# Placing attention units, token mixing and loads among MLP matmuls by planned matmul time, and beginning the second batch's units while its loads still arrive

## Chip, cores and metric

The kernel runs on one core of one Trainium2 chip. The metric is device time in microseconds (us), the median over several runs. Every kernel is compared with the kernel before on the same chip.

## The reference

Four batches of 768 tokens, 8 heads of 48, so a model width of 384. First a decaying attention:

```python
for t in range(S):
    kt, vt, rt = (k[:, :, t], v[:, :, t], r[:, :, t])
    cur = np.einsum('bhd,bhe->bhde', u[None] * kt, vt)
    y[:, :, t] = np.einsum('bhd,bhde->bhe', rt, state + cur)
    state = w[None, :, :, None] * state + np.einsum('bhd,bhe->bhde', kt, vt)
```

Then a mixer: one product over tokens (hidden width 256), one over channels (hidden width 1536), each with a residual:

```python
xt = x.transpose(0, 2, 1)
h = np.maximum(xt @ w_tok1, 0.0) @ w_tok2
u = x + h.transpose(0, 2, 1)
h2 = np.maximum(u @ w_ch1, 0.0) @ w_ch2
return (u + h2)
```

Token mixing needs all 768 tokens of a batch, so the channel MLP of a batch cannot begin before the attention of that whole batch is done.

## The kernel before

The attention goes in 24 "units" of 128 tokens: units 0 to 5 are batch 0, 6 to 11 batch 1, and so on. A unit passes through four stages, one per "slot". Slot `s` runs them for four neighbouring units, so that each engine has another unit's work while one waits:

```python
STAGES = ((3, stage_c), (2, stage_b), (1, stage_a), (0, stage_p))

def slot(s, lo, hi):
    for lag, f in STAGES:
        if lo <= s - lag < hi:
            f(*units[s - lag])
```

The profile calls the engines PE (TensorE, the matrix products), DVE (VectorE), ACT (ScalarE), POOL (GpSimd) and SP (SyncE, which here issues the loads, the stores and the transposing DMAs). In the timelines PE's products and the operations of DVE, ACT and POOL start in the order in which the Python code calls these functions, so this order is the schedule of each engine. The lines, by stage:

```python
# stage_p (units of batch 1 on): POOL, POOL, ACT, POOL
pool.tensor_mul(kp[:, :, 0:D], h3(kt), h3(wn[:, g, :]))      # `dve if early` cut
pool.tensor_mul(rp[:, :, 0:D], h3(rt), h3(wp[:, g, :]))
act.copy(vb, vt)
pool.tensor_mul(ku, kt, u_bc)
# stage_a: eight transposes on PE (cut), then
act.copy(L["rk"], tr_ps)
dve.tensor_mul(rku, L["ku"], L["rt"])
dve.tensor_reduce(adg, h3(rku), axis=mybir.AxisListType.X, op=ALU.add)
# stage_b: yd on POOL, eight products on PE (cut), two mask products AT on DVE (cut)
pool.tensor_mul(h3(L["yd"]), h3(L["vb"]), L["adg"].unsqueeze(2).to_broadcast([128, H, D]))
# stage_c: products into y_ps and kv_ps on PE (cut), then the state S and x_b on DVE (cut)
```

So POOL has four products a slot (yd, kp, rp, ku), and DVE has rku, adg, two AT, S and x_b, seven operations with an osb or a u_sb where one falls into the slot. Token mixing, the two MLP halves, and their DVE parts:

```python
def back(c):
    hT_ps = psM.tile([128, dm], f32, name="hT_ps", tag="m")
    for i in range(2):
        pe.matmul(hT_ps, wtok2[:, i, ts(c, 128)], h1r[:, i, :], start=(i == 0), stop=(i == 1))
    dve.tensor_add(u_sb[:, c, :], x_b[:, c, :], hT_ps)
    if not by_pe:
        sp.dma_start_transpose(uT[:, :, ts(c, 128)], u_sb[:, c, :])

def up(b, sg, jt):      # cut: three matmuls of uT into z_ps (tag "m"), then
    return act.activation(zr[:, jt, :], z_ps, Relu)

def down(b, sg, si):    # cut: twelve matmuls of zr into h2_ps (tag "m"), then
    dve.tensor_add(osb, mixed[b][0][:, c, :], h2_ps)
    sp.dma_start(out[b, ts(c, 128), :], osb)
```

All of z_ps, h_ps, hT_ps and tr_ps share one ring of four buffers (tag "m") in PSUM, where PE's products are written. A matmul group that opens a new buffer waits until DVE or ACT has read the one four places back.

For the first batch's MLP the order was a list of ups and downs with hand-set positions:

```python
items = ([None] * 6 + ups[6:16] + [downs[0]] + ups[16:20] + [downs[1]] + ups[20:] + downs[2:5] + [None])
slot_at = dict(zip(range(6, 16), (14, 17, 19, 21, 23, 25, 26, 27, 28, 28)))
load_at = (1, 3, 5, 7, 9, 11, 18, 20, 22, 24, 25, 26, 27)
tok_at = (28, 29, 29)
```

Slot 7, the first with a transpose of batch 1, stands behind ten ups and a down: ups[6:16] are items 6 to 15, the down is item 16, and slot 7 goes ahead of item 17.

## Time and profile before

| | before |
|---|---|
| median of 3 timed runs | 190.89 us (190.28 to 191.17) |
| span of the profiled run | 188.6 us, mean clock 0.98 |
| PE busy | 163.5 us (87%), 1434 instructions |
| DVE / ACT / POOL busy | 116.9 (62%) / 87.3 (46%) / 95.2 (50%) us |
| first up of batch 1, 2, 3 | 90.20, 125.61, 157.60 us |
| end of PE | 185.1 us |

The shares are averages over stages with different limits, so the row to read is the time of the first up of batch 1: ahead of it PE has gaps, from there on it has almost none.

### The profile page before, as it was taken

To read this page: it belongs to the slowest core of one execution; us is meant where nothing else is said; L and a number is where in the kernel's file an instruction comes from. 1 tells how busy PE (TensorE), PEld (TensorE's weight loads), DVE (VectorE), ACT (ScalarE), POOL (GpSimd) and SP (SyncE) were. 2 spreads that over 40 slices of the span, in tenths; PEclk is the share of its full clock that TensorE was granted. 3 is DMA by queue.
4 is the path that set the end of the run, shared out by engine and by line. 5 is a ranking of instruction groups with operands and counts; after the bars stand their busy time and mean duration, and the time that the engine had idled before them with its cause. 6 is when DMAs were issued, how large, how long until landed. Compare 5 with 4: busy or idle time off the path is not lost.

```text
span 188.6 us, 3783 instructions
## 1 busy us (share of the span) xinstructions
PE 163.5 (87%) x1434; PEld 104.4 (55%) x1434; DVE 116.9 (62%) x204; ACT 87.3 (46%) x168; POOL 95.2 (50%) x114
## 2 busy tenths in 40 slices
PE   5456579899998696895899999899999999999992
PEld 2255465366665464553666666466666666666661
DVE  4599997430599999939577874967765261111121
ACT  4933341479575344313556653534454525445510
POOL 5799998700299999966456772656410000000000
PEclk9999999999999999589999999999999999999999
DMA  6999999997999979404399744232011124211112
GB/s 128 215 191 218 180 211 199 186 188 149 222 222 213 215 157 239 105 0 104 66 217 200 159 114 100 71 70 80 0 45 42 42 48 116 92 42 45 73 52 83
DMA packets 90070, 24.03 MB, mean 127 GB/s; under 512 B 83267, under 2 KB 90053, under 8 KB 90053
## 3 DMA queue, kind: packets, MB, share of 16 engines
q1 hardware_dynamic: 86240, 20.65, 50.7%
q0 software_dynamic: 3808, 3.15, 10.7%
q8 instruction: 11, 0.18, 0.4%
q14 instruction: 7, 0.05, 0.1%
q10 hardware_dynamic: 4, 0.00, 0.0%
HBM read 20.45 MB, written 4.72 MB: 133 GB/s over the span
## 4 chain that ended last, share of the span: by engine, by line
PE 54%; SPq 19%; POOL 10%; DVE 6%; issue 4%; DMA 3%; ACT 1%; POOLq 0%; DVEq 0%
PE h_ps L68 26%; SPq L68 19%; PE z_ps L68 18%; PE tr_ps L68 3%; POOL yd L68 2%; PE y_ps L68 2%; POOL rp_129 L68 2%; DVE u_sb L68 2%; PE hT_ps L68 2%; POOL kp_130 L68 2%; DMA vt<-in_v_dram 2%; DMA uT<-u_sb 1%; DVE rku L68 1%; POOL rp_125 L68 1%; POOL rp_121 L68 1%
## 5 line engine op out<-in xcount | busy, mean ns | idle before, releaser
L68 ACT ACTIVATE zr<-z_ps 128x384 bf16<-128x384 f32 x96 | 43.9, 495 | 26.1 <-PE z_ps L68 26.1
L68 PE MATMUL z_ps<-uT,wch_149 128*128 128x384 bf16 x288 | 52.0, 326 | 3.2 <-DMA uT<-u_sb 2.7
L68 PE MATMUL h_ps<-wch_150,zr 128*128 128x384 bf16 x288 | 50.5, 326 | 0.0
L68 ACT COPY rk<-tr_ps 128x1024 bf16<-128x1024 bf16 x24 | 24.3, 1012 | 53.0 <-PE tr_ps L68 52.7
L68 DVE TENSOR_TENSOR osb<-u_sb,h_ps 128x384 f32<-128x384 bf16 x24 | 13.3, 553 | 50.8 <-PE h_ps L68 50.8
L68 PEld LDWEIGHTS <-zr 128*128 128x128 bf16 x288 | 28.1, 98 | 19.4 <-issue 1.5
L68 PEld LDWEIGHTS <-wch_149 128*128 128x128 bf16 x288 | 27.3, 98 | 20.0 <-issue 3.6
L68 POOL TENSOR_TENSOR yd<-vb,adg 128x384 f32<-128x384 bf16 x24 | 20.7, 862 | 28.8 <-DVE adg L68 16.4
L68 DVE TENSOR_TENSOR rku<-ku,rt 128x384 f32<-128x384 f32 x24 | 25.5, 1060 | 1.6 <-POOL ku L68 1.6
L68 POOL TENSOR_TENSOR ku<-kt,u_bc 128x384 f32<-128x384 f32 x24 | 24.5, 1022 | 0.0
L68 PEld LDWEIGHTS <-rk 48*128 48x128 bf16 (+1 forms) x272 | 12.5, 105 | 6.2 <-ACT rk L68 2.8
L68 DVE TENSOR_REDUCE adg<-rku 128x8 f32<-128x384 f32 x24 | 13.3, 553 | 0.8
L68 ACT CAST vb<-vt 128x384 bf16<-128x384 f32 x24 | 12.3, 513 | 0.0
L68 PE MATMUL hT_ps<-h1r,wtok_148 128*128 128x384 bf16 x48 | 9.4, 325 | 0.8 <-ACT h1r L68 0.4
L68 POOL TENSOR_TENSOR rp_121<-rt,wp 128x384 bf16<-128x384 f32 x8 | 8.9, 1112 | 2.3 <-ACT wp L68 2.3
L68 POOL TENSOR_TENSOR kp_126<-kt,wn 128x384 bf16<-128x384 f32 x6 | 6.0, 996 | 6.5 <-issue 5.9
L68 POOL TENSOR_TENSOR rp_129<-rt,wp 128x384 bf16<-128x384 f32 x8 | 8.9, 1114 | 0.0
L68 POOL TENSOR_TENSOR rp_125<-rt,wp 128x384 bf16<-128x384 f32 x8 | 8.6, 1073 | 0.0
L68 PEld LDWEIGHTS <-wtok_147 128*128 128x128 bf16 x48 | 5.6, 120 | 5.1 <-issue 3.5
L68 POOL TENSOR_TENSOR kp_122<-kt,wn 128x384 bf16<-128x384 f32 x6 | 6.0, 997 | 4.3 <-issue 3.6
L68 ACT ACTIVATE h1r<-h_ps 128x384 bf16<-128x384 f32 x8 | 3.5, 488 | 9.3 <-PE h_ps L68 9.3
L68 PEld LDWEIGHTS <-wtok_148 128*128 128x128 bf16 x48 | 4.7, 98 | 4.5 <-issue 1.8
(306 smaller groups left out, 231.5 us busy)
## 6 DMA issues: line engine op xcount, KB each, us to landing
kt<-in_k_dram SPq DMA_DIRECT2D x24, 192.0 KB, 3.6
rt<-in_r_dram SPq DMA_DIRECT2D x24, 192.0 KB, 3.7
vt<-in_v_dram SPq DMA_DIRECT2D x24, 192.0 KB, 3.7
out_dram<-osb SPq DMA_DIRECT2D x24, 192.0 KB, 2.0
wch_149<-in_moe_w_ch_dram POOLq DMA_DIRECT2D x3, 384.0 KB, 8.6
wch_150<-in_moe_w_ch_dram POOLq DMA_DIRECT2D x1, 1152.0 KB, 16.7
wtok_147<-in_moe_w_tok_dram POOLq DMA_DIRECT2D x1, 384.0 KB, 7.8
wtok_148<-in_moe_w_tok_dram POOLq DMA_DIRECT2D x1, 384.0 KB, 7.1
```

The lines of the kernel that those rows point to most:

```text
L68: return lambda *args, **kw: tc.keep_in_program_order(f(*args, **kw))
```

## The change

The intent: give every piece a planned PE cost (an up 0.5 us, a down 2.0, a slot 1.4), and give each slot, mixing step and load a planned time at which it is set among the ups and downs. In the stretch of batch 0's MLP, slots 6, 7 and 8 now come first, while the loads of their units still arrive; the slots follow every 4.2 planned us; mixing of batch 1 is split into its hidden product (H) and two halves of the second product (K1, K2) with slots between them; and one slot and one down more are done before batch 1's first up. Positions in the later batches change too. No operation is added or removed. The core of the diff:

```diff
-            items = ([None] * 6 + ups[6:16] + [downs[0]] + ups[16:20] + [downs[1]] + ups[20:] + downs[2:5] + [None])
-            slot_at = dict(zip(range(6, 16), (14, 17, 19, 21, 23, 25, 26, 27, 28, 28)))
-            load_at = (1, 3, 5, 7, 9, 11, 18, 20, 22, 24, 25, 26, 27)
-            tok_at = (28, 29, 29)
 ... (the loop that walked these positions, removed)
+    def merge(items, events):
+        now, events = 0.0, sorted(events, key=lambda e: e[0])
+        for cost, f in items:
+            while events and events[0][0] <= now:
+                _, c, g = events.pop(0)
+                g()
+                now += c
+            f()
+            now += cost
+        for _, _, g in events:
+            g()
+    UP, DOWN, SLOT = 0.5, 2.0, 1.4
 ... (helpers att, mixing, ups, downs, woven, fetch)
+    u1 = ups(0, 1)
+    items = ups(0, 0, 6) + u1[:6] + downs(0, 0, 0, 1) + u1[6:] + downs(0, 0, 1) + downs(0, 1)
+    events = [att(0.0, 6), att(0.0, 7), att(1.5, 8)] + [att(6.0 + 4.2 * j, 9 + j) for j in range(6)]
+    events += mixing(1, 27.5, 30.0, 32.0) + [att(29.0, 15), att(31.0, 16)]
+    merge(items, fetch([0.0] * 6 + [12.0, 16.0, 20.0, 24.0, 26.0, 27.0]) + events)
+    for b in range(1, B):
+        dn = downs(b - 1, 1) if b > 1 else []
+        items = (woven(ups(b, 0), dn) if dn else ups(b, 0)) + woven(ups(b, 1), downs(b, 0))
+        span = sum(c for c, _ in items)
+        events = []
+        if b + 1 < B:
+            at = [0.0, 5.5, 11.0, 16.0, 22.0, 28.0] if b == 1 else [0.0, 6.0, 12.0, 18.0]
+            events += [att(t, (17 if b == 1 else 23) + j) for j, t in enumerate(at)]
+            total = span + 4.0 + SLOT * len(at)
+            events += mixing(b + 1, total - 8.0, total - 4.5, total - 2.0)
+            events = fetch([0.0, 5.0, 10.0, 15.0, 20.0, 25.0]) + events
+        merge(items, events)
```

The stretch is written as a list of words, in the order in which the functions are called: S6 is slot 6, U4 four ups, D a down, H, K1 and K2 as above; loads are left out of the lists. The two kernels are:

```
before:  U8 S6 U2 D S7 U2 S8 U2 S9 D U1 S10 U2 S11 U1 S12 D S13 D S14 S15 H D K1 K2
changed: S6 S7 S8 U4 S9 U6 S10 U2 D S11 U5 S12 U1 D D S13 D S14 H S15 K1 S16 K2 D D
```

More of the change, by code (lines that the diff above doesn't have):

```diff
@@ L378 @@
         tn[3 + c]()
-    for b in range(B):
-        if b == 0:
-            ups = [lambda jt=jt, sg=sg: up(0, sg, jt) for sg in range(2) for jt in range(NJ)]
-            downs = [lambda sg=sg, si=si: down(0, sg, si) for sg in range(2) for si in range(3)]
-            items = ([None] * 6 + ups[6:16] + [downs[0]] + ups[16:20] + [downs[1]] + ups[20:] + downs[2:5] + [None])
-            slot_at = dict(zip(range(6, 16), (14, 17, 19, 21, 23, 25, 26, 27, 28, 28)))
-            load_at = (1, 3, 5, 7, 9, 11, 18, 20, 22, 24, 25, 26, 27)
-            tok_at = (28, 29, 29)
-        else:
-            items = []
-            for sg in range(2):
-                for si in range(3):
-                    if sg == 1 or b > 1 or si == 2:
-                        items.append(lambda si=si, b=b, sg=sg: down(b - 1 + sg, 1 - sg, si))
-                    items += [lambda jt=4 * si + j, sg=sg, b=b: up(b, sg, jt) for j in range(4)]
-            m = len(items)
-            slot_at = {6 * b + 10 + j: m - 30 + 5 * j + 1 for j in range(6)}
-            if b == 1:
-                slot_at[16] = 0
-            load_at = range(0, m, 5)
-            tok_at = (m - 8, m - 5, m - 2)
-        toks = None
-        for n in range(len(items)):
-            for x in load_at:
-                if x == n:
-                    load_next()
-            for s, x in slot_at.items():
-                if x == n:
-                    slot(s, C, len(units))
-            if b + 1 < B:
-                if n == tok_at[0]:
-                    toks = token_mix(b + 1)
-                    for f in toks[0]:
-                        f()
-                if n == tok_at[1]:
-                    for f in toks[1][:3]:
-                        f()
-                if n == tok_at[2]:
-                    for f in toks[1][3:]:
-                        f()
-            if items[n]:
-                items[n]()
@@ L422, with att @@
-    for si in range(3):
-        down(B - 1, 1, si)
+    def merge(items, events):
[10 more added lines that the diff above has]
+    UP, DOWN, SLOT = 0.5, 2.0, 1.4
+    def att(t, s):
+        return (t, SLOT, lambda: slot(s, C, len(units)))
@@ new lines, in mixing, with ups, downs, woven @@
+    def mixing(b, t_hid, t_bk1, t_bk2):
+        hid, bk, _ = token_mix(b)
+        go = lambda fs: [f() for f in fs]
+        return [(t_hid, 2.0, lambda: go(hid)), (t_bk1, 1.0, lambda: go(bk[:3])),
+                (t_bk2, 1.0, lambda: go(bk[3:]))]
+    def ups(b, sg, lo=0, hi=NJ):
+        return [(UP, lambda jt=jt: up(b, sg, jt)) for jt in range(lo, hi)]
+    def downs(b, sg, lo=0, hi=3):
+        return [(DOWN, lambda si=si: down(b, sg, si)) for si in range(lo, hi)]
+    def woven(us, ds):
+        out = []
+        for i, d in enumerate(ds):
+            out += [d] + us[4 * i:4 * i + 4]
+        return out
@@ new lines, in fetch @@
+    def fetch(times):
+        return [(t, 0.0, load_next) for t in times]
+    u1 = ups(0, 1)
[15 more added lines that the diff above has]
+        merge(items, events)
@@ L425 @@
+    for _, f in downs(B - 1, 1):
+        f()
 _INS = ['r', 'k', 'v', 'w', 'u', 'moe_w_tok1', 'moe_w_tok2', 'moe_w_ch1', 'moe_w_ch2']
```

## The prediction

> **What bounds the kernel now.** I read the page first, then the busy time by stretch, the chain of waits, and the timeline of POOL. Some names for pieces of work, by the tiles that they write: an "up" is three matmuls into z_ps, a "down" is twelve of zr into h_ps, A is the eight transposes of a unit into tr_ps, B its eight products into at_ps, C its state and output products into y_ps and kv_ps. Units 0 to 5 belong to batch 0, 6 to 11 to batch 1, and so on. A slot s does C of unit s-3, B of s-2, A of s-1, and P of s (the products kp, rp, ku on POOL).
>
> ```profile
> PE   5456579899998696895899999899999999999992
> POOL 5799998700299999966456772656410000000000
> PEclk9999999999999999589999999999999999999999
> DMA  6999999997999979404399744232011124211112
> ```
>
> The reader sees three regimes. The DMA is full until about 75 us, PE has gaps until about 90 us, and from there PE is full to the end. POOL stops for some 14 us at slices 8 to 10 (counted from 0) and is then full.
>
> ```profile
> core 0: us, PE busy (x) PEld busy (x) DVE busy (x) ACT busy (x) POOL busy (x), PEclk, DMA share, GB/s
> 41.70:53.70 12.00, 11.50 (x107) 7.27 (x105) 4.46 (x8) 10.01 (x22) 3.14 (x4) 1.00 0.98 190
> 53.70:77.50 23.80, 18.63 (x233) 12.74 (x233) 23.59 (x39) 10.40 (x17) 23.80 (x25) 0.95 0.99 210
> 77.50:90.20 12.70, 9.93 (x72) 5.91 (x73) 9.79 (x19) 3.72 (x6) 8.58 (x9) 0.82 0.16 41
> 90.20:185.10 94.90, 94.01 (x778) 59.27 (x778) 47.89 (x84) 44.47 (x91) 27.83 (x30) 1.00 0.35 85
> ```
>
> From 53.7 to 77.5 us POOL is busy 23.80 of 23.80 us, and DVE 23.59. Before that POOL has only 3.14 of 12.00.
>
> ```profile
> 35.55 0.99 POOL L68 TENSOR_TENSOR ku<-kt,u_bc 128x384 f32<-128x384 f32 x1
> 50.56 0.83 POOL L68 TENSOR_TENSOR yd<-vb,adg 128x384 f32<-128x384 bf16 x1 [14.03 <-DVE adg L68]
> 51.35 1.00 POOL L68 TENSOR_TENSOR kp_130<-kt,wn 128x384 bf16<-128x384 f32 x1
> 52.31 1.32 POOL L68 TENSOR_TENSOR rp_129<-rt,wp 128x384 bf16<-128x384 f32 x1
> 53.59 1.00 POOL L68 TENSOR_TENSOR ku<-kt,u_bc 128x384 f32<-128x384 f32 x1
> 54.55 0.83 POOL L68 TENSOR_TENSOR yd<-vb,adg 128x384 f32<-128x384 bf16 x1
> ```
>
> This is the costliest wait for the path: POOL stands in program order at yd of unit 6, which wants adg. The DVE pair that makes adg stands behind the first osb, so behind the first down, which PE ends at 48.7 us. From then on a slot takes four POOL products, and the starts of yd lie 54.55 - 50.56 = 3.99 us apart, with six more starts at 58.52, 62.49 up to 78.39: 3.97 each.
>
> ```profile
> 76.20 1.28 POOL rp_129 L68
> 77.52 0.61 PE tr_ps L68 x4
> 78.13 5.86 PE h_ps L68 x24
> 84.01 0.55 DVE osb L68
> 84.57 2.07 DVE u_sb L68 x5
> ...
> 87.72 2.34 DMA uT<-u_sb
> 90.07 0.14 issue
> 90.20 2.11 PE z_ps L68 x12
> ```
>
> The chain of waits shows what POOL's pace costs: PE waits for rp of unit 14, only then mixes batch 1, all six u_sb follow in one piece, then the transposing DMAs, and PE stands from about 87.5 to 90.2 us. From 90.2 us to 185.1 us PE is the bound.
>
> **What the Trainium skill says.** "SBUF — State Buffer", section "Who interferes with whom": a DVE instruction with two SBUF inputs contends with a POOL instruction that reads SBUF, and the second one blocks fully. The trace agrees: rku, two f32 inputs, takes 0.55 us at 49.25 with POOL idle and 1.34 us in most slots of the full stretch; rp there takes 1.28 instead of 0.96 us. So POOL and DVE cannot be counted as independent. "Perfetto Trace Analysis", section "Per-instruction lifecycle", GPSIMD part, advises to time POOL by start-to-start spacing, which I do. "TensorE: Matmul & The Clock Gate", Part 1, says that an idle window drops PE to half clock; here the clock is 0.82 in the stretch 77.5 to 90.2 and the 24 matmuls of the chain take 5.86 us where 24 take 3.9 us later. "DMA: Bandwidth & Descriptors", Specifications, wants runs of at least 512 B for line rate; the page has 83267 of 90070 packets under 512 B and about 200 GB/s while full, so I take the loads' landing times as they are.
>
> **The change, part by part.** No operation is added or removed; the order listing has the same number of instructions on every engine. Up to the last transpose of batch 0 (about 41.7 us on PE) the streams are the same.
>
> 1. Start of batch 1. Before, PE runs ten ups and a down ahead of A6. After, PE goes on with A6, B6, A7, four ups, then slot 9. On DVE rku and adg of unit 6 come right after the u_sb of batch 0, which end at 39.4 us, with no osb ahead. So yd6 is over by about 42 us. But the next POOL product is kp of unit 8, and its load is not there: by the completion times in the trace kt, rt and vt of unit 8 land at 45.1, 45.8, 46.6 us, unit 9 by 49.4, 10 by 52.2, 11 by 54.7. So kp8 starts at 45.1 instead of 51.35: POOL's pipeline moves forward by 6.2 us, not by the 14 us of the wait. After that loads (2.7 us a unit) are faster than POOL (3.97 us a slot). The load order up to unit 11 is unchanged.
>
> 2. PE's work in the stretch from 41.7 us to the first up of batch 1. Durations from the chain of waits: four ups 1.95, so 0.49 each; a down 1.95; C 0.54, B 0.33, A 0.55 (starts 92.31, 92.85, 93.18, 93.73); twelve matmuls of a first mixing product 1.95, three pairs of a second 0.97. Before, the stretch holds 18 ups (8.8), 5 downs (9.8), 10 A, 9 B, 8 C (12.8) and the mixing (3.9): 35.3 us of work in 90.2 - 41.7 = 48.5 us, so 13.2 us are gaps and half clock. After, it holds 18 ups, 6 downs (11.7), 11 A, 10 B, 9 C (14.2) and the mixing: 38.6 us.
>
> 3. How long it takes after. POOL's slots start at 48.2 + 3.97 (s - 9). I walk down PE's order with that, with the four buffers of the "m" psum ring, and with DVE at 0.47 to 0.6 us an operation: A8 at 47.6, A9 at 52, A10 56.4, A11 60.3, two downs to 64.7, A12 66.1, A13 69.5, first mixing product to 71.5, A14 73, three second products to 73.9, C13 waits for its mask product on DVE until 74.3, A15 waits for rp15 until 75.1. The last three second products and the first of two downs reach 79.4. The second down needs the psum of a second product, which DVE frees only after rku15 and adg15, at about 81.1, so it ends at 83.1, and slot 17 at 84.5. The transposing DMAs of the first three blocks are long done (u_sb at 77, landing about 81). So the first up of batch 1 is at 84.5, and 84.5 - 41.7 - 38.6 = 4.2 us of gaps are left.
>
> 4. The rest. Before, from 90.2: 72 ups (35.1), 19 downs (37.1), 8 A, 9 B, 10 C (12.8), two mixings (7.8): 92.8 us in 94.9, so 2.1 us of stalls. After: 72 ups, 18 downs (35.2), 7 A, 8 B, 9 C (11.3), two mixings: 89.4 us. The slots are set 4 to 6 us apart there, but for slots 22 and 23, with three second products and slot 22 between; DVE and POOL have half of the stretch free. I keep 2 us of stalls, and 3.5 us for the tail after PE.
>
> Sum: 84.5 + 89.4 + 2.1 + 3.5 = 179.5 us of span. The timed median is 2.3 us over the span of 188.6, so 181.8. The same from the difference: 13.2 - 4.2 = 9.0 us off 190.9 is 181.9. I round to 181.7.
>
> **Rivals.** (a) DVE becomes the bound. DVE was already at 23.59 of 23.80; after, six u_sb and six osb lie in the same stretch as the slots. For: in every slot with an osb DVE has almost no slack. Against: rku's 1.34 us is partly a wait for POOL, and slots with an osb kept 3.97. If every one of those twelve (0.47 each) pushed PE, 5.6 us come back: 186 to 187. (b) PE takes over at once and POOL's pace is hidden: 38.6 us without gaps, 177.6 us. For it: PE is then 90% loaded in the walk. (c) Loads hold it: the loads of units 12 on stand behind output stores in SP's order, which wait for osb. Against: at 3.97 us a slot unit 15 is wanted at 73 us, and the walk has it landed at about 71; at most 1 to 2 us. (d) The stretch loses to a drop of the PE clock: fewer gaps speak against it; one window as before would cost about 2 us. (e) Nothing gained, because the end is PE bound: no, since PE's gaps ahead of 90.2 us are a part of that sum.
>
> **Range and chances.** Rival (b) sets the low end, (a) with some of (c) the high end: 177.5 to 186.5. Faster by over 2% needs less than 187.1: 0.90. Within 2%: 0.08, if (a) and (c) come together. Slower: 0.02.
>
> **What would show it.** POOL's long wait of 14 us shrinks to under 4 us before yd6 plus a wait of some 3 us for kt before kp8 at about 45 us. The starts of yd are still near 4 us apart, from 48 to about 76. The first up of batch 1 comes at 82 to 87 us instead of 90.2, with one down and one slot more done. PE's clock stays near 1.00 from 42 to 85. From there to PE's end 90 to 93 us. I am wrong if yd's spacing grows past 4.3 us (DVE), if kp8 starts at 51 again (loads), or if the second half has over 4 us of stalls.

## The result

| | before | changed |
|---|---|---|
| median, us (4 runs of each) | 190.9 (190.28 to 191.17) | 185.47 (184.84 to 185.77) |
| profiled span, us | 188.6 | 183.1 |
| PE busy | 163.5 (87%) | 159.7 (87%) |
| DVE busy | 116.9 (62%) | 116.4 (64%) |
| POOL busy | 95.2 (50%) | 94.9 (52%) |
| first up of batch 1 | 90.20 | 86.76 |
| end of PE | 185.1 | 179.6 |

The ratio is 0.9716, with a 95% interval of 0.9679 to 0.9753: faster by 2.8%. Ratios here are the mean time of one kernel's fast runs over that of the other's of the same rounds, so they are not quite the ratio of the medians quoted. Executions over 1.5% slower than the fastest of the same kernel are left out of the means. PE's lower busy time is not less work: it has the same 1434 instructions, but the half-clock stretch from 75.1 to 82.0 us of the kernel before is gone.

Is the gain only this clock? By the record it can be a part, not all. Of the eleven runs of the kernel before that were made beside e5, those with a mean clock of 0.987 or 0.988 took 189.78 to 190.15 us, those with 0.980 to 0.982 took 190.62 to 191.46: about 1 us apart, for means that differ by one stretch of 3.4 us at half clock. By this estimate the 6.9 us above are worth some 2 of the 5.4 us. The four runs of the changed kernel have 0.988 to 0.999, and the one with the lowest clock is the fastest (184.84).

The slices of the changed kernel (one digit per 1/40 of the span, busy tenths; the last row the granted PE clock):

```profile
PE   5556579996999999677999999799999997999992
POOL 5799898905998877983668864770100000000000
PEclk9999999999999999999999999999999999999998
```

POOL's hole is now slice 8 and half of slice 9, and the clock is full up to PE's end. PE is still weak in slices 16 to 18 (6, 7, 7), which are 73 to 87 us. The same table of windows as before, with the two last edges moved to the new first up and the new end of PE:

```profile
core 0: us, PE busy (x) PEld busy (x) DVE busy (x) ACT busy (x) POOL busy (x), PEclk, DMA share, GB/s
41.70:53.70 12.00, 10.32 (x125) 7.21 (x124) 8.20 (x14) 10.28 (x21) 10.47 (x11) 1.00 1.08 207
53.70:77.50 23.80, 22.68 (x270) 15.69 (x268) 21.42 (x36) 11.65 (x23) 20.23 (x22) 1.00 0.83 176
77.50:86.80 9.30, 6.63 (x63) 4.24 (x63) 8.46 (x17) 1.41 (x2) 6.03 (x7) 1.00 0.27 55
86.80:179.60 92.80, 90.36 (x737) 56.83 (x734) 46.13 (x80) 45.35 (x91) 26.40 (x29) 1.00 0.38 93
```

From 53.7 to 77.5 PE now does 22.68 of 23.80 us (18.63 before) and POOL has slack (20.23). But from 77.5 to 86.8 PE is busy for only 6.63 of 9.30 us at full clock, while DVE is busy 8.46. POOL's timeline (start, duration, engine, operation, then in brackets the idle time before it and what ended that):

```profile
35.57 0.99 POOL L68 TENSOR_TENSOR ku<-kt,u_bc 128x384 f32<-128x384 f32 x1
43.23 0.83 POOL L68 TENSOR_TENSOR yd<-vb,adg 128x384 f32<-128x384 bf16 x1 [6.67 <-ACT vb L68]
44.02 1.00 POOL L68 TENSOR_TENSOR kp_130<-kt,wn 128x384 bf16<-128x384 f32 x1
...
66.14 1.00 POOL L68 TENSOR_TENSOR kp_126<-kt,wn 128x384 bf16<-128x384 f32 x1 [1.11 <-issue]
...
70.23 0.83 POOL L68 TENSOR_TENSOR yd<-vb,adg 128x384 f32<-128x384 bf16 x1 [1.17 <-DVE adg L68]
```

The wait of 14.03 us before yd of unit 6 has become one of 6.67, and what ends it is no longer adg from DVE but vb from ScalarE. ScalarE makes vb of unit 6 at 42.57 us, behind the last copy into uT, which starts at 42.21. kp of unit 8 starts at 44.02 without waiting: its load had landed at 42.7 in this run (45.1 in the profile before). yd then starts at 47.21, 51.19, 55.20, 60.22, 64.20, 70.23, 74.21, 78.18 and 83.05. Three spacings, 5.02, 6.03 and 4.87, are well over four us. DVE's timeline around the second:

```profile
65.70 0.55 DVE L68 TENSOR_TENSOR osb<-u_sb,h_ps 128x384 f32<-128x384 bf16 x1 [1.27 <-PE h_ps L68]
...
68.30 1.17 DVE L68 TENSOR_TENSOR rku<-ku,rt 128x384 f32<-128x384 f32 x1
69.50 0.55 DVE L68 TENSOR_REDUCE adg<-rku 128x8 f32<-128x384 f32 x1
```

Two downs stand in PE's order ahead of slot 13, so DVE gets the osb of each; at the second it is idle for 1.27 us waiting for PE, and S, x_b, two AT and then rku and adg stand behind it. adg is done at 70.05, so yd starts at 70.23 after 1.17 us of idle POOL. Work that POOL needs waits behind work that PE has not finished. A single down can do the same on a smaller scale: ahead of the spacing of 5.02, DVE waits 0.73 us for the down at 55.70. From the second osb on DVE has hardly a pause (the window has the columns of the table above; DVE's busy time is the third):

```profile
65.70:84.70 19.00, 15.23 (x177) 10.19 (x174) 18.86 (x32) 6.57 (x10) 15.39 (x16) 1.00 0.63 136
```

DVE is busy for 18.86 of 19.00 us, so each result there comes as late as all of DVE's work ahead of it makes it. On PE, close to the first up, that looks like this:

```profile
78.46 1.27 PE L68 MATMUL hT_ps<-h1r,wtok_148 128*128 128x384 bf16 x6 [1.06 <-DVE u_sb L68]
79.57 2.11 PE L68 MATMUL h_ps<-wch_150,zr 128*128 128x384 bf16 x12
83.39 2.11 PE L68 MATMUL h_ps<-wch_150,zr 128*128 128x384 bf16 x12 [1.71 <-DVE u_sb L68]
```

K2 (78.46) and then the second of the last two downs (83.39) wait 1.06 and 1.71 us for u_sb on DVE: going back four places in the PSUM ring, their buffers are those of the first products of K1 and of K2, which DVE has not yet read. (Gaps quoted below are counted from start to start, less the usual spacing; these two are then 1.23 and 1.87.) The chain of waits says the same from the other end:

```profile
81.46 0.84 DVE rku L68
...
82.79 0.56 DVE u_sb L68
...
83.39 2.11 PE h_ps L68 x12
```

DVE has rku, adg, u_sb in this order without a pause (rku 81.38 to 82.29, u_sb from 82.79), and PE starts its down right after the first u_sb. In the kernel before this part of the chain went through POOL's rp, then the half-clock downs and the transposing DMAs.

### The profile page after: what moved, and what is told of

It reads as the page before. It is cut to its first block, busy times and chain, and to the rows that moved or that the text cites.

```text
span 183.1 us, 3782 instructions
## 1 busy us (share of the span) xinstructions
PE 159.7 (87%) x1434; PEld 103.2 (56%) x1434; DVE 116.4 (64%) x204; ACT 87.5 (48%) x168; POOL 94.9 (52%) x114
## 4 chain that ended last, share of the span: by engine, by line
PE 70%; DVE 14%; ACT 4%; DMA 3%; issue 3%; SPq 1%; POOL 1%; DVEq 0%; POOLq 0%; ACTq 0%
PE h_ps L68 30%; PE z_ps L68 24%; PE tr_ps L68 4%; PE y_ps L68 3%; DVE rku L68 3%; PE hT_ps L68 3%; DVE u_sb L68 2%; DMA vt<-in_v_dram 2%; DMA kt<-in_k_dram 2%; PE kv_ps L68 1%; SPq L68 1%; ACT zr L68 1%; DVE x_b_151 L68 1%; PE w_ps L68 1%; ACT h1r L68 1%
## 5 line engine op out<-in xcount | busy, mean ns | idle before, releaser
L68 ACT ACTIVATE zr<-z_ps 128x384 bf16<-128x384 f32 x96 | 43.4, 498 | 31.1 <-PE z_ps L68 31.1
L68 PEld LDWEIGHTS <-wch_149 128*128 128x128 bf16 x288 | 27.4, 98 | 19.0 <-issue 2.4
L68 POOL TENSOR_TENSOR ku<-kt,u_bc 128x384 f32<-128x384 f32 x24 | 26.7, 1114 | 0.0
L68 DVE TENSOR_TENSOR rku<-ku,rt 128x384 f32<-128x384 f32 x24 | 24.7, 1028 | 1.6 <-POOL ku L68 1.6
L68 POOL TENSOR_TENSOR rp_121<-rt,wp 128x384 bf16<-128x384 f32 x8 | 8.0, 997 | 2.3 <-ACT wp L68 2.3
L68 POOL TENSOR_TENSOR rp_129<-rt,wp 128x384 bf16<-128x384 f32 x8 | 8.0, 996 | 0.0
L68 POOL TENSOR_TENSOR rp_125<-rt,wp 128x384 bf16<-128x384 f32 x8 | 8.0, 996 | 0.0
L68 PEld LDWEIGHTS <-wtok_148 128*128 128x128 bf16 x48 | 4.6, 99 | 5.1 <-issue 2.9
L68 POOL TENSOR_TENSOR kp_122<-kt,wn 128x384 bf16<-128x384 f32 x6 | 6.0, 996 | 2.8 <-PE kv_ps L68 2.8
L68 POOL TENSOR_TENSOR kp_126<-kt,wn 128x384 bf16<-128x384 f32 x6 | 6.0, 996 | 2.7 <-issue 2.3
L68 POOL TENSOR_TENSOR kp_130<-kt,wn 128x384 bf16<-128x384 f32 x6 | 6.0, 999 | 2.2 <-issue 2.1
```

Of the source, the lines that this page charges most:

```text
L68: return lambda *args, **kw: tc.keep_in_program_order(f(*args, **kw))
```

## The experiments

Every kernel has a profile and timed runs beside the kernel before on the same chip: three rounds for the first four (kernel before 190.04 us), five for the others (kernel before 190.65 us in both groups).

My theory after the result: the gain is in the stretch up to batch 1's first up, and what is left there (about 2.3 us against the prediction) is DVE's order, the prediction's rival (a). Rivals: the gain comes from placing the later batches; it comes from splitting the mixing rather than from the early begin; the remaining gaps come from PE's own order or the fill at 42 us.

### e1: the new stretch alone

```diff
-        items = (woven(ups(b, 0), dn) if dn else ups(b, 0)) + woven(ups(b, 1), downs(b, 0))
 ... (the planned times of b = 1, 2, 3, removed; the loop of the kernel before, put back with three changes:)
+                if (sg == 1 or b > 1 or si == 2) and not (b == 1 and sg == 0):
+            del slot_at[16]
+            slot_at = {s: max(x, 1) for s, x in slot_at.items()}
```

The changes leave out slot 16 and the down that the new stretch has already done.

> The changed order up to the mixing of batch 1, the order of before from batch 1's ups on. If the gain is made in the stretch before batch 1's first up: 184.5 to 186.5 us, as the whole change. If the later placing carries a good part: 188 or more.

Measured: 183.79 us (183.66 to 184.15), ratio 0.9685 [0.9647, 0.9722]; first up of batch 1 at 85.61. This is 0.7 us under the range that I had expected. The new stretch alone has all of the gain; the interval overlaps that of the changed kernel.

### e2: the new later placing alone

The stretch is the old list; the loops for b = 1 on are the new ones, with slot 16 and the last down of batch 0 put back into them.

```diff
-        items = (woven(ups(b, 0), dn) if dn else ups(b, 0)) + woven(ups(b, 1), downs(b, 0))
+        us = ups(b, 0)
+        items = (woven(us, dn) if dn else us[:8] + downs(0, 1, 2) + us[8:]) + woven(ups(b, 1), downs(b, 0))
-            at = [0.0, 5.5, 11.0, 16.0, 22.0, 28.0] if b == 1 else [0.0, 6.0, 12.0, 18.0]
+            at = [0.0, 1.0, 7.0, 12.5, 18.0, 24.0, 30.0] if b == 1 else [0.0, 6.0, 12.0, 18.0]
```

> The order of before up to batch 1's mixing, the changed order from batch 1's ups on (one more slot there). If the gain is made before batch 1's first up: 190 to 192 us, as before. If the later placing carries it: 188 or less.

Measured: 189.57 us (188.85 to 190.65), ratio 0.9991 [0.994, 1.0043]. The later placing carries nothing that these runs resolve. With e1 this settles where the gain is.

### e3: the split mixing without the early begin

```diff
-S6 S7 S8 U4 S9 U6 S10 U2 D S11 U5 S12 U1 D D S13 D S14 H S15 K1 S16 K2 D D
+U8 S6 U2 D S7 U2 S8 U2 S9 D U1 S10 U2 S11 U1 S12 D S13 D S14 H S15 D K1 S16 K2 D
```

> The changed kernel, but batch 1's units begin after ten ups and a down as before; its mixing stays split among slots. If the early begin makes the gain (POOL's products of unit 8 at 44 instead of 51 us): 189 to 191 us, with kp of unit 8 at 51 us again. If the split mixing makes it: under 187 us.

Measured: 186.29 us (185.83 to 186.44), ratio 0.9809 [0.9771, 0.9848]; kp of unit 8 at 51.22 as in the kernel before, first up at 87.87. I missed by some 3 us: I had put nearly all of the gain on the early begin, and the other branch, under 187 us, came true. (Whether e3 is faster than the kernel before by the full 2% is unclear: the interval holds 0.98.) This kernel also keeps the one slot and the one down more before the first up, so its gain is that of the split mixing and of these two together. The window of this kernel (from:to length, then busy time of PE, PEld, DVE, ACT, POOL, clock, DMA share, GB/s) shows that POOL's pace is as it was:

```profile
53.70:77.50 23.80, 19.69 (x248) 13.48 (x247) 23.59 (x39) 11.13 (x19) 23.80 (x25) 1.00 0.93 195
```

POOL is busy 23.80 of 23.80 us, as before. What this kernel gains lies after 77.5 us: with slots 15 and 16 and a down between H, K1 and K2, PE has work while POOL finishes, and PE's clock did not drop in the profiled run (mean 0.999).

### e4: the early begin without the split mixing

```diff
-... S13 D S14 H S15 K1 S16 K2 D D
+... S13 D S14 S15 H D K1 K2 S16 D
```

> The changed kernel with its early begin, but batch 1 is mixed in one piece after unit 14's transposes, as before. If the early begin makes the gain: within 1.5 us of 185.5. If the split makes it: 188 to 190, with PE standing for 2 to 3 us at the transposing DMAs before batch 1's first up.

Measured: 184.77 us (183.28 to 185.03, 5 runs), ratio 0.9741 [0.9697, 0.9784]; first up at 84.06 in the profile. So with the early begin, splitting the mixing brings nothing that these runs resolve. This list also takes the last two downs apart (see e9), so it does not undo the split alone. e3 saves 190.04 x (1 - 0.9809) = 3.6 us, e4 saves 190.04 x (1 - 0.9741) = 4.9, and both together 190.9 x (1 - 0.9716) = 5.4: the parts do not add. As I read it, both fill the same hole ahead of the first up.

### e5: control

The changed kernel again, unedited, beside the next three.

> The changed kernel itself, unchanged, as the measure for the three runs beside it on the same chip: ratio to before 0.968 to 0.975.

Measured: fast runs 184.92 to 185.83 us, ratio 0.9733 [0.9698, 0.9767].

### e6: the last mixing half moved behind the waiting place

```diff
-... S15 K1 S16 K2 D D            (then batch 1: S17 U3 ...)
+... S15 K1 S16 D D               (then batch 1: S17 U3 K2 ...)
```

> The changed kernel with the last three second products of batch 1's mixing moved from before the pair of downs to behind slot 17 and three ups. If PE's two gaps of 1.2 and 1.9 us at 77 and 81 us are psum waits on DVE, which stands at the products of units 14 and 15: both go, 2 to 3 us faster than the control. If DVE's total work bounds the stretch: same within 0.7 us, the gaps come back elsewhere.

Measured: 185.38 us (183.51 to 185.86), ratio 0.9713 [0.9674, 0.9752], the same as the control. A wait moved: now the downs wait for the u_sb that K2 waited for. PE's timeline of this kernel, the two last downs in one row:

```profile
79.34 5.33 PE L68 MATMUL h_ps<-wch,zr 128*128 128x384 bf16 x24 [1.06 <-DVE u_sb L68]
```

The second gap is gone, but the 24 matmuls took 5.33 us where such a row takes 4.06 at full clock (e8): in the profiled run the clock was at half from 78.5 to 81.9. That cannot be the whole reason, since another run with mean clock 0.999 took 185.43 us (and one at 1.00 took 183.51). So the second branch of the expectation came true, the one for DVE's total work as the bound: the same time, with the wait at another place. How much the clock took is open.

### e7: the pair of downs pulled apart, with a slip

```diff
-S12 U1 D D S13 D S14 H S15 K1 S16 K2 D D
+S12 U1 D S13 D S14 D H S15 K1 S16 K2 D
```

> The changed kernel with the two pairs of downs taken apart, one of each moved one or two slots. If the pair ahead of slot 13 is what breaks POOL's pace (yd 64.20 to 70.23) and that pace matters: 1 to 2 us faster than the control. If PE, not POOL, is the bound in that part: POOL's pace gets even, the time stays within 0.7 us.

One of six downs was left out, so one block of the output was never written and the result is wrong (not a number). It took 182.57 us with less work; nothing is concluded from it. e9 repeats it in full.

### e8: six additions of batch 1 taken from DVE

x_b is added on PE, by a third accumulating matmul with the identity, and ScalarE copies the sum out, for batch 1's mixing only:

```diff
-                pe.matmul(hT_ps, wtok2[:, i, ts(c, 128)], h1r[:, i, :], start=(i == 0), stop=(i == 1))
-            dve.tensor_add(u_sb[:, c, :], x_b[:, c, :], hT_ps)
+                pe.matmul(hT_ps, wtok2[:, i, ts(c, 128)], h1r[:, i, :], start=(i == 0), stop=(i == 1 and b != 1))
+            if b == 1:
+                pe.matmul(hT_ps, ident, x_b[:, c, :], start=False, stop=True)
+                act.copy(u_sb[:, c, :], hT_ps)
+            else:
+                dve.tensor_add(u_sb[:, c, :], x_b[:, c, :], hT_ps)
```

> The changed kernel with the six u_sb of batch 1 taken from DVE: PE adds x_b by an identity product (six more matmuls, 1.0 us) and ScalarE copies. If DVE is the bound in the stretch (rival a): PE's gaps at 77 and 81 us shrink by 2.5 us or more, 1.5 to 2.5 us faster than the control net. If DVE is not: 1 us slower.

Measured: 181.56 us (180.81 to 181.79), ratio 0.9523 [0.9493, 0.9553], correct. It is the fastest of all, 4.0 us under the control's fast median of 185.54, where I had expected 1.5 to 2.5. PE around the place of the two waits:

```profile
78.69 0.33 PE L68 MATMUL hT_ps<-x_b,ident 128*128 128x384 bf16 x1
78.85 4.06 PE L68 MATMUL h_ps<-wch,zr 128*128 128x384 bf16 x24
```

The last identity matmul and both downs follow without a gap, and the downs run at full clock (4.06 us for 24). The first up comes at 84.17 instead of 86.76, though PE does about 1 us more work (six matmuls of 0.16 us each), and from the first up to PE's end it takes 91.7 instead of 92.8 us. So it was DVE that held PE ahead of the first up; that is shown, not only argued. The 1.1 us after the first up are not explained by this: there PE's gap of 1.48 us at 150.5 is 0.40 here, in a batch that the edit leaves alone.

POOL's pace, on the other hand, is not what e8 repaired. Its yd starts at 64.09 and then at

```profile
70.39 0.83 POOL L68 TENSOR_TENSOR yd<-vb,adg 128x384 f32<-128x384 bf16 x1 [1.17 <-DVE adg L68]
```

That is a spacing of 6.30, and yd of unit 14 starts at 78.34 (78.18 in the changed kernel). With POOL as late as before, the first up still comes 2.6 us sooner. What cost that time was PE's wait for buffers that DVE had yet to read, and not the break in POOL's pace.

### e9: the pair of downs pulled apart, all six

```diff
-S12 U1 D D S13 D S14 H S15 K1 S16 K2 D D
+S12 U1 D S13 D S14 D H S15 K1 D S16 K2 D
```

> The run with split downs again: the earlier one had lost a down by a slip of mine (so its last output rows of batch 0 were never written, and it saved 1.95 us of PE work). Now all six are there, one ahead of each slot. If the pair ahead of slot 13 sets the time through POOL's pace: 1.5 to 3 us faster than the changed kernel (ratio to before 0.957 to 0.964). If PE's work alone is the bound there: POOL's pace gets even at about 4 us, the ratio stays at 0.970 to 0.974.

Measured: 182.70 us (181.52 to 183.98), ratio 0.9589 [0.9551, 0.9627]; first up at 83.70, although in this run its loads came some 2 us later (kp of unit 8 at 45.89). POOL:

```profile
65.55 0.83 POOL L68 TENSOR_TENSOR yd<-vb,adg 128x384 f32<-128x384 bf16 x1 [1.18 <-DVE adg L68]
...
69.52 0.82 POOL L68 TENSOR_TENSOR yd<-vb,adg 128x384 f32<-128x384 bf16 x1
...
73.49 0.83 POOL L68 TENSOR_TENSOR yd<-vb,adg 128x384 f32<-128x384 bf16 x1
```

From 65.55 to 77.47 the spacing is 3.97 or 3.98. One wait of 1.18 us for adg is left before it (the spacing there is 4.87) and one of 1.27 after it (4.97); the 6.03 is gone. Same operations, other order, and 185.54 - 182.70 = 2.8 us less by the medians of two groups of runs, on two chips that gave the kernel before the same 190.65.

The time is what the first branch expected, but the run does not show that branch's cause, for it took both pairs of downs apart. yd of unit 14 starts at 77.47, only 0.7 us sooner than in the changed kernel, while the first up comes 3.1 us sooner. On PE the last down now follows its mixing half like this:

```profile
80.33 2.11 PE L68 MATMUL h_ps<-wch,zr 128*128 128x384 bf16 x12 [0.18 <-ACT rk L68]
```

With one down ahead of slot 16 and one behind K2, the buffer four places back is that of slot 16's transposes, which ScalarE has read about 2 us before DVE reaches the first u_sb of K2 (82.18). The waits of 1.06 us ahead of K2 and of 1.71 us ahead of the last down are both gone. A run with only the pair ahead of slot 13 pulled apart was not made, so what that pair is worth is open. The profiled run is the slowest of the six; from its first up to PE's end it takes 94.6 us.

### e10: ups moved into the fill

```diff
-S6 S7 S8 U4 S9 U6 S10 U2 D ...
+S6 S7 U2 S8 U2 S9 U6 S10 U2 D ...
```

> The changed kernel with two of the four ups set between unit 6's transposes and its products, where PE stands 1.83 us for ScalarE's copies of batch 1's first unit. If a gap of PE is worth its length: 1.0 to 1.8 us faster (ratio 0.963 to 0.968). If POOL or DVE hold the stretch anyway: same as the changed kernel, 0.970 to 0.974.

Measured: 184.98 us (184.14 to 186.83), ratio 0.9715 [0.9671, 0.9759]: no different from the control. The gap of 1.83 us at 42.2 on PE shrinks to 0.86, and a new one of 1.36 opens at 49.35. ScalarE shows why:

```profile
49.92 0.51 ACT L68 CAST vb<-vt 128x384 bf16<-128x384 f32 x1 [0.94 <-DMA vt<-in_v_dram]
50.34 2.39 ACT L68 ACTIVATE zr<-z_ps 128x384 bf16<-128x384 f32 x6
```

vb of unit 9 waits for its load, and six zr stand behind it, whose PSUM buffers the next ups need. What is pulled ahead waits later. In part this is the run: the load came at about 49.9 us here and had landed at 48.2 in the changed kernel's profile.

### e11: mixing of batches 2 and 3 moved

K2 goes behind the next batch's first down, and batch 3's H comes 2 planned us earlier.

```diff
-            events += mixing(b + 1, total - 8.0, total - 4.5, total - 2.0)
+            m3 = mixing(b + 1, total - (8.0 if b == 1 else 10.0), total - (4.5 if b == 1 else 6.9), 3.4)
+            events += m3[:2]
 ... (m3[2:] is set among the next batch's events)
```

> The changed kernel with the mixings of batches 2 and 3 moved: their last three second products behind the first down of the next batch, and batch 3's first product two us earlier. The gaps of 1.2 us at 117 us (psum behind DVE) and 1.5 us at 150 us (transposing DMA) should both go: 1.5 to 2.7 us faster than the changed kernel (ratio 0.958 to 0.965). If they come back at another place: 0.970 to 0.974.

Measured: 187.01 us (185.84 to 188.13), ratio 0.9823 [0.9781, 0.9866]: slower than the changed kernel (0.9716 and, as the control, 0.9733), a miss. The gap at 150.5, for a late transposing DMA, is gone, but another came on PE:

```profile
119.49 1.14 PE L68 MATMUL hT_ps<-h1r,wtok 128*128 128x384 bf16 x6
122.63 1.62 PE L68 MATMUL z_ps<-uT,wch 128*128 128x384 bf16 x9 [2.00 <-DVE osb L68]
```

PE has its K1 at 119.49 and can open the next buffer only after an osb that stands behind rku and adg in DVE's order (osb at 122.03). It is the same fault as in the first stretch, moved to another batch.

### e12: all of it together

e8's additions, e9's spread downs, a fill much like e10's and e11's mixing:

```diff
-S6 S7 S8 U4 S9 U6 S10 U2 D S11 U5 S12 U1 D D S13 D S14 H S15 K1 S16 K2 D D
+S6 S7 U2 S8 U3 S9 U5 S10 U3 D S11 U5 S12 D S13 D S14 D H S15 K1 D S16 K2 D
```

> All together: six u_sb of batch 1 by PE and ScalarE, ups filled in at unit 6, downs one by one, mixings of batches 2 and 3 moved. If the parts add: 177.5 to 180 us, ratio 0.930 to 0.945. If the u_sb relief already holds most of what the split downs and the fill give: 0.940 to 0.950.

Measured: fast runs 181.23 to 183.84 us (one slow run left out), ratio 0.9566 [0.9521, 0.9611]: missed, and no better than e8. The first up comes at 82.88, the earliest of all, but the rest takes 95.3 us instead of e8's 91.7: it has e11's wait again, and a half-clock window from 118.7 to 122.1. e8 with e9's order and without e11's mixing was not run, so whether these two add up is open.

## Why the prediction was right or wrong

The call, faster by over 2%, was right; 185.47 lies in the range, 3.8 us over the point.

**What bounds it, and where the gain is: right.** e1 has all of the gain in the stretch up to the first up, e2 has none after it. The first up came at 86.76, between the predicted 82 and 87, with full clock.

**Step 1, the early begin: right in kind; that it went further than forecast is luck.** POOL went forward by 51.35 - 44.02 = 7.3 us instead of 6.2. Two parts differ. The load of unit 8 landed at 42.7, not 45.1, so kp did not wait for it; that is the run and not the order, since kp of unit 8 waits for its load until 44.99 in e8 and 45.89 in e9. And yd of unit 6 was not over at 42 but started at 43.23, because vb stood behind ScalarE's copies, which I had not looked at; so the wait before it was 6.67 us and not under 4. What the step was worth I had not separated: e3 shows that without it two thirds of the gain are there (3.6 of 5.4 us), with the split mixing and the one slot and down more, and e4 that with it the split adds nothing resolved.

**Step 2, the work of 38.6 us: borne out as far as the order goes.** The instruction counts are the same and 86.76 - 41.7 - 38.6 leaves 6.5 us of gaps.

**Step 3, the walk: its gap term failed, 4.2 predicted and 6.5 measured.** The walk was at most 0.8 us early up to the first three second products (done at 73.9 in the walk, at 74.3 on PE). Then C13 got its last mask product from DVE at 76.16 instead of 74.3, and from there the walk was right in kind and 2 us early: it had the last down wait for u_sb of DVE until 81.1, and it waited until 83.39. So the term that was too small is DVE's time. The walk counted DVE at 0.47 to 0.6 us an operation, though the prediction itself had read 1.34 us for rku in most slots: the four rku from 68.30 to 82.29 took 1.17, 1.29, 1.35 and 0.91 us, 4.7 us where the walk allowed at most 2.4. And it did not have the 1.27 us in which DVE stood at 65.70 for the second of two downs. How much of the 2.3 us each of the two made, no run separates.

The sign that the prediction named, yd's spacing past 4.3 us, came true: (83.05 - 43.23) / 9 = 4.42 on the average. POOL was 2.2 us behind the line 48.2 + 3.97 (s - 9) at 70.23 (68.05 on the line). But that break is in e8 too, and there the first up comes at 84.17, close to the predicted 84.5: the break was a sign of DVE's lateness and not what PE paid for. So rival (a), DVE, was there in part. Six of its twelve additions, taken away in e8, are worth 4.0 us of the timed median, and e9 gains 2.8 with an order in which, among other things, PE's last down no longer needs a buffer of theirs. The rival's own sum is off: 181.7 + 5.6 is 187.3, not 186 to 187.

**Step 4, the rest: 1.3 us more.** The work of 89.4 us and the tail of 3.5 us held. 92.84 us were taken, so 3.4 us of stalls and not 2.1. The two largest single gaps are 1.18 us at 117.2, for u_sb of batch 2 on DVE, and 1.48 us at 150.5, by my reading for the third transposing DMA of batch 3: it landed at 152.02, and PE starts at 152.11. (The profile names osb, which was done at 151.39; this up reads no osb, and its buffer is not that of the down before it.)

**The sum.** 2.3 (step 3) + 1.3 (step 4) = 3.6 us: the span was 183.1 for 179.5 predicted.

**Rivals (b) to (e).** (b), PE without gaps, did not come: its 177.6 us were missed by 7.9. (c), the loads, did not hold the stretch in this run; their landing differed by 2 to 3 us between runs. (d), a clock drop, did not come in the profiled run; those of e6, e10 and e12 had one. (e) is refuted by the result.

## What to carry to other kernels

When one piece of work is moved ahead, follow the order of every engine behind it to the end, and add up each engine's work there with the durations that it has when the others are busy too (rku took 0.55 us with POOL idle, 1.17 to 1.35 in the late slots). Then ask of each group on PE which buffer it takes over and who has to read that buffer first: with both downs behind K2, the last one waited 1.71 us for DVE, with one of them ahead of slot 16 it waited 0.18 us for ScalarE. Work that two changes hide under the same hole doesn't add up (3.6 and 4.9 us made 5.4), so undo each alone before crediting one. Moving a piece past its wait gave the wait a new place in e6, e10 and e11; taking work off the engine that is waited for (e8), or spreading the downs so that PE no longer needs its buffers at once (e9), made it shorter.

## What the Trainium skill lacked or had wrong

- "TensorE: Matmul & The Clock Gate", Part 1, ties the drop to an idle window of about 3.4 us; it also tells of drops from frequent short pauses, without a measure for them. Two half-clock windows of 3.4 us followed 3.4 us in which PE was busy for 2.19 us (e6, window from 75.1) and 1.84 us (e10, from 75.8), with no gap over about 1.4 us; in the changed kernel 3.4 us with 1.69 us busy (from 80.2) and a gap of 1.87 were followed by none. How much of a window may be idle isn't stated there, and these runs do not settle it: where no drop came, the place of the window is not known.
- "DMA: Bandwidth & Descriptors", section "Latency and other measured facts", gives 261 GB/s for transposing DMAs, measured on one kernel. Here six of 128 x 384 bf16 (98,304 bytes each), from SBUF to SBUF on one queue, occupied the queue for 7.76 us in the kernel before (from 85.06), 1.29 us each, which is 76 GB/s, with a median of 2.4 us from issue to landing. The section has no time for a small transpose; in the kernel before PE waits 2.75 us for these ahead of its first up at 90.20.
